# Nine changes of order and shape in a hand-scheduled attention-plus-mixer kernel

## The chip, the cores and the metric

The kernel runs on one core of one Trainium2 chip. The metric is device microseconds of one execution. A core has TensorE (PE; its weight loads are listed apart as PEld), VectorE (DVE), ScalarE (ACT), GpSimd (POOL) and SyncE (SP), which here only issues DMAs. Each engine works through its own list in order and waits on semaphores for the others.

## The reference

`B, H, S, D = 8, 8, 576, 64`, all inputs float32.

```python
def phi(x, c, s):                       # c, s: cos and sin of pi/2 * position / S
    r = np.maximum(x, 0.0)
    return np.concatenate([r * c, r * s], axis=-1)
q_p, k_p = phi(q, cos_w, sin_w), phi(k, cos_w, sin_w)
kv  = np.einsum('bhsf,bhsd->bhfd', k_p, v)
num = np.einsum('bhsf,bhfd->bhsd', q_p, kv)
den = np.einsum('bhsf,bhf->bhs', q_p, np.sum(k_p, axis=2))[..., None] + 1e-06
x   = (num / den).transpose(0, 2, 1, 3).reshape(B, S, H * D)      # 8 x 576 x 512

wq, wk = x @ w_q, x @ w_k                                        # 512 -> 64
W_tok  = 1 / np.sqrt(64) * np.einsum('bsd,btd->bst', wq, wk)
mixed  = np.einsum('bst,btd->bsd', W_tok, x)
out    = np.maximum(mixed, 0.0) @ w_out                          # 512 -> 512
```

The mixer is computed as wq times (wk-transposed times x), so that no 576 x 576 matrix is formed.

## The kernel before, in words

A batch is worked on in two *halves* of four heads, so there are 16 halves, H = 0 to 15; batch b has halves 2b and 2b+1. A half has two head pairs, and its results come in two groups g = 2H and 2H+1.

The program is one list of words, `ORDER`, read from left to right. Each word is one step, and its function has the word's letters as its name. A number behind the letters is the half, the group, the batch or the output tile; `a` and `b` are the two parts of a half; `:n` is the PSUM bank (of 8) that the step writes; `@A`, `@V`, `@G` put it on ACT, DVE or POOL. Nothing reorders the list: each engine gets its steps in the order of the list, and the framework adds the semaphore waits that data and buffers need. So a word further ahead on one engine changes nothing on another engine but what waits there.

The steps of a half, in the order of the data:

- `LK`, `LQ`, `LV` load k, q and v to five raw buffers each, all on SP's one queue, 288 KB a part. At most eight DMAs are on their way: a new one waits for the eighth before it. `ST` stores an output tile of 256 KB on the same queue, so a store whose tile isn't ready holds up the loads behind it.
- `RK`, `RQ` apply relu and give bf16. `CV` casts v, and `VS` (DVE) multiplies it with the cos/sin table; `VG` does both on POOL.
- `KV` sums k-transposed times v on PE, `KE` copies the sum to SBUF.
- `QT` transposes q on PE: for the halves in `QT_WIDE` with 9 transposes of 128 x 128, for the others with 18 of 64 rows by 64. `QM` (DVE) multiplies the result with the table into the operand of `N`: two instructions for a wide half, one for another.
- `N` multiplies with the sum of `KV` (20 small matmuls a group; five groups add epsilon with two more, line 348). `EP` adds epsilon, `RC` and `RJ` take reciprocals, `X` (DVE) writes x.
- `XT` (10 transposes of 128 x 128) or `XR` (20 of 64 rows) transposes x on PE, `XE` copies it out.

The steps of a batch: `WK`, `KW` (x times w_k and its copy), `WQ`, `QW` (the same for w_q), `KX`, `XK`, `XA`, `XB` (wk-transposed times x, its copy, and two copies across partitions), `MX`, `ME` (the mixing and its relu, four tiles a batch). Two batches give nine output tiles: `WO` (4 matmuls of 512 columns, line 509), `OE` (copy to SBUF), `ST`.

A `:n` of `QT`, `KV`, `N`, `XT`, `XR` and `MX` stands for the pair of banks n and n+1; `WK`, `WQ`, `KX` and `WO` take one bank. A step that writes a bank waits until the step that read its last content is done; so the bank number decides which engine a PE step waits for.

## Time and profile before

| | |
|---|---|
| median of 3 runs | 119.17 us (118.6 to 119.84) |
| the profiled execution | 118.42 us, of which the profile's span is 116.6 us; 1.8 us lie around it |
| PE busy | 94.7 us, 81% of the span, 2104 matmuls |
| DVE busy | 90.5 us, 78%, 162 instructions |
| ACT busy | 83.1 us, 71%, 147 instructions |
| POOL busy | 64.8 us, 56%, 65 instructions |
| DMA | 39.38 MB, mean 338 GB/s; loads 29.62 MB, stores 9.44 MB |
| granted TensorE clock | 0.9 or more in all 40 slices |

No engine is busy all the time. The page cuts the span in 40 slices of 2.9 us; in most of them two engines show eight tenths or more, and the DMA engines are at nine tenths in most of the first half. The chain of work that ended last tells which of them sets the end at each time; the timeline shows, for each instruction, how long its engine sat idle before it and who released it.

### The profile page before, as it was taken

To read this page: it belongs to the slowest core of one execution; us is meant where nothing else is said; L and a number is where in the kernel's file an instruction comes from. 1 tells how busy PE (TensorE), PEld (TensorE's weight loads), DVE (VectorE), ACT (ScalarE), POOL (GpSimd) and SP (SyncE) were. 2 spreads that over 40 slices of the span, in tenths; PEclk is the share of its full clock that TensorE was granted. 3 is DMA by queue.
4 is the path that set the end of the run, shared out by engine and by line. 5 is a ranking of instruction groups with operands and counts; after the bars stand their busy time and mean duration, and the time that the engine had idled before them with its cause. 6 is when DMAs were issued, how large, how long until landed. Compare 5 with 4: busy or idle time off the path is not lost.

```text
span 116.6 us, 4971 instructions
## 1 busy us (share of the span) xinstructions
PE 94.7 (81%) x2104; PEld 65.1 (56%) x2118; DVE 90.5 (78%) x162; ACT 83.1 (71%) x147; POOL 64.8 (56%) x65
## 2 busy tenths in 40 slices
PE   0005967779796797999999899999999999999970
PEld 0004856657576776647775656656775576463420
DVE  2008999799798999889799887898997996795620
ACT  4547558499899987898884878986888774546340
POOL 7600399861634796477298498899659901002000
PEclk9999999999999999999999999999999999999999
DMA  3999999999999999999979999987898467999874
GB/s 90 349 386 399 401 372 346 388 389 396 386 392 384 387 387 387 391 390 384 383 251 302 351 397 371 358 266 258 270 340 293 169 236 271 403 367 400 337 306 173
DMA packets 20662, 39.38 MB, mean 338 GB/s; under 512 B 3232, under 2 KB 3232, under 8 KB 20640
## 3 DMA queue, kind: packets, MB, share of 16 engines
q1 hardware_dynamic: 20640, 39.07, 92.4%
q8 instruction: 16, 0.26, 0.9%
q14 instruction: 6, 0.05, 0.1%
HBM read 29.62 MB, written 9.44 MB: 335 GB/s over the span
## 4 chain that ended last, share of the span: by engine, by line
PE 48%; DMA 26%; DVE 14%; SPq 4%; issue 3%; ACT 1%; DVEq 0%; ACTq 0%
PE ps L509 24%; DMA qraw<-in_q_dram 16%; DMA vraw<-in_v_dram 5%; DMA kraw<-in_k_dram 5%; PE ps L340 5%; DVE qm L316 5%; SPq L145 4%; PE ps L285 3%; PE ps L489 3%; PE ps L419 3%; PE ps L439 3%; DVE xT L213 3%; PE ps L466 3%; PE ps L452 2%; DVE x L393 2%
## 5 line engine op out<-in xcount | busy, mean ns | idle before, releaser
L248 POOL TENSOR_TENSOR v<-vraw,vtab 128x1152 bf16<-128x1152 f32 (+1 forms) x12 | 35.5, 2969 | 6.5 <-DVE qm L316 2.2
L509 PE MATMUL ps<-wow,mix 128*128 128x512 bf16 x130 | 33.3, 380 | 1.2 <-issue 0.3
L393 DVE TENSOR_TENSOR x<-ps,rec 128x640 bf16<-128x640 f32 x32 | 25.4, 818 | 0.7
L209 ACT COPY o<-ps 128x512 f32<-128x512 f32 x25 | 14.5, 592 | 9.2 <-PE ps L509 8.1
L509 PEld LDWEIGHTS <-mix 128*128 128x128 bf16 x144 | 12.5, 98 | 14.4 <-issue 1.7
L295 PE MATMUL ps<-ident,rq 128*128 128x128 bf16 x117 | 9.5, 233 | 12.0 <-ACT rq L203 11.0
L316 DVE TENSOR_TENSOR qm<-ps,qtab 128x1152 bf16<-128x1152 bf16 x26 | 18.3, 749 | 0.8 <-PE ps L295 0.7
L234 DVE TENSOR_TENSOR v<-vb,vtab 128x2304 bf16<-128x2304 bf16 (+1 forms) x11 | 11.8, 1084 | 7.7 <-ACT vb L209 7.3
L500 ACT ACTIVATE mix<-ps 128x576 bf16<-128x576 f32 x23 | 14.5, 651 | 3.5 <-PE ps L489 2.5
L340 PE MATMUL ps<-kvs,qm 64*128 64x65 bf16 x640 | 14.0, 193 | 2.1 <-ACT kvs L209 1.3
L295 PEld LDWEIGHTS <-rq 128*128 128x128 bf16 x117 | 7.6, 104 | 13.6 <-issue 10.5
L340 PEld LDWEIGHTS <-qm 64*128 64x128 bf16 x640 | 12.6, 96 | 4.2 <-issue 2.3
L203 ACT ACTIVATE rk<-kraw 128x1152 bf16<-128x1152 f32 (+1 forms) x14 | 14.0, 996 | 0.7 <-DMA kraw<-in_k_dram 0.7
L205 POOL TENSOR_SCALAR rq<-qraw 128x576 bf16<-128x576 f32 (+1 forms) x13 | 10.1, 776 | 4.4 <-DMA qraw<-in_q_dram 3.5
L211 POOL TENSOR_SCALAR vb<-vraw 128x576 bf16<-128x576 f32 (+1 forms) x7 | 5.7, 810 | 11.9 <-DMA vraw<-in_v_dram 8.8
L211 POOL TENSOR_SCALAR kx<-kx 64x256 bf16<-64x256 bf16 x9 | 4.1, 457 | 12.6 <-ACT kx L209 11.0
L502 DVE TENSOR_SCALAR mix<-ps 128x576 bf16<-128x576 f32 x9 | 6.8, 757 | 4.0 <-PE ps L489 3.8
L285 PE MATMUL ps<-v,rk 64*64 64x130 bf16 x432 | 9.1, 231 | 0.8 <-POOL v L248 0.7
L209 ACT CAST kvs<-ps 128x260 bf16<-128x260 f32 (+1 forms) x15 | 6.5, 436 | 4.6 <-PE ps L285 3.9
L285 PEld LDWEIGHTS <-rk 64*64 64x64 bf16 x432 | 7.5, 114 | 3.9 <-issue 1.2
L203 ACT ACTIVATE rq<-qraw 128x576 bf16<-128x576 f32 (+1 forms) x10 | 8.3, 832 | 1.1 <-DMA qraw<-in_q_dram 1.1
L213 DVE COPY xT<-ps 128x1280 bf16<-128x1280 bf16 (+1 forms) x9 | 7.3, 813 | 2.2 <-PE ps L419 2.0
(65 smaller groups left out, 137.3 us busy)
## 6 DMA issues: line engine op xcount, KB each, us to landing
kraw<-in_k_dram SPq DMA_DIRECT2D x32, 288.0 KB, 5.9
qraw<-in_q_dram SPq DMA_DIRECT2D x32, 288.0 KB, 5.9
vraw<-in_v_dram SPq DMA_DIRECT2D x32, 288.0 KB, 5.8
out_dram<-o SPq DMA_DIRECT2D x36, 256.0 KB, 3.4
wof<-in_moe_w_out_dram SPq DMA_DIRECT2D x4, 256.0 KB, 5.8
wkf<-in_moe_w_k_dram SPq DMA_DIRECT2D x1, 128.0 KB, 5.7
wqf<-in_moe_w_q_dram SPq DMA_DIRECT2D x1, 128.0 KB, 6.2
```

The costliest lines, as they stand in the source:

```text
L203: A.activation(dst, s, AF.Relu)
L209: A.copy(dst, s)
L213: V.tensor_copy(dst, s)
L234: V.tensor_mul(v2_b[H % NV2][:, part, :, :, 0:D], vb_b[H % NPREP][:, part].unsqueeze(3).to_broadcast([P, n, C, 2, D]), vtab.unsqueeze(1).t ...
L248: G.tensor_mul(dst[:, part, :, :, 0:D], s[:, part].unsqueeze(3).to_broadcast([P, n, C, 2, D]), vtab.unsqueeze(1).to_broadcast([P, n, C, 2, ...
L285: nc.tensor.matmul(kv_v[o, r, :], rk_of(H)[a, pr, c, :], v2_b[H % NV2][a, pr, c, :, 0:D + 1], start=(c == 0), stop=(c == C - 1))
L295: nc.tensor.transpose(qt_v[:, c, :], rq_b[H % NPREP][:, c, :, :], ident)
L316: V.tensor_mul(qm_b[H % NQM][:, :, r, 0:C, :], q_t[:, r].unsqueeze(1).to_broadcast([P, 2, C, H2]), qtab)
L340: nc.tensor.matmul(nv[:, pr, u, :], qm_b[H % NQM][a, s, r, 2 * u:2 * u + 2, :], kv_b[H % 2][a, r, pr if H in KV_WIDE else 0, s, 0:D + 1], ...
L393: V.tensor_tensor(x_b[b % NX][:, :, 4 * h:4 * h + 4, :].rearrange("p u (w r) d -> p r w u d", r=2)[:, r], nv[:, :, :, 0:D], rec(g).to_broa ...
L500: A.activation(dst, s, AF.Relu, scale=scale_moe)
L509: nc.tensor.matmul(o, mix_b[bp % 2][:, m, rt * P:(rt + 1) * P], wow[:, m, :], start=(m == 0), stop=(m == NDM - 1))
```

## The change

Nine edits, all in the list but the one in `QT_WIDE`:

1. `XR0:4` becomes `XT0:4`: 10 full transposes in place of 20 small ones for half 0.
2. `VS7` (one DVE instruction for both parts) becomes `VS7b VS7a` (two, the part that POOL casts first).
3. `WK2` moves from behind `N14` to ahead of `MX3` and `N14`, from bank 6 to bank 2. For this, `MX3` goes from bank 2 to 0, `N14` from 0 to 6, `WQ2` from 7 to 3, `KV6` from 2 to 0, and `N12` ahead of `N13`.
4. `MX9` moves behind `N16`.
5. `LQ12a` moves behind `ST11` on SP's queue.
6. `OE11` moves from DVE to ACT.
7. `XA3` and `QM11` move behind `KE11`, `XR9` and `XE8`; `XR9` goes from bank 4 to 0; `WO10` moves from ahead of `KV11` to behind `QT10`, from bank 1 to 4; `MX13` and `MX12` change banks.
8. `QT10` is no longer wide: 18 small transposes in place of 9, and `QM10` is one instruction.
9. `WK6` moves behind `WO25`, `KW6` behind `OE25`.

The line with most of the seventh edit, and the line of the eighth:

```diff
-LQ12b QT11:4 OE5:5@A RC19 RC18 X18 WO9:0 X19 WO10:1 OE9:7@A RQ10@G KV11:2 XA3@A QM11 XR8:6 KE11@A
-XR9:4 VG10a LV15a LV13a LQ14b LV14b LQ14a LV13b XE8@A QT10:2 XE9@V WO0:5 QM10 OE10:8@A MX13:0
+LV12b LK12b LQ12b QT11:4 OE5:5@A RC19 RC18 X18 WO9:0 X19 OE9:7@A RQ10@G KV11:2 XR8:6 KE11@A XR9:0
+VG10a LV15a LV13a LQ14b LV14b LQ14a LV13b XE8@A XA3@A QM11 QT10:2 WO10:4 XE9@V WO0:5 QM10 OE10:8@A
...
-    QT_WIDE = (0, 1, 2, 3, 4, 5, 6, 7, 8, 9, 10, 11, 14)
+    QT_WIDE = (0, 1, 2, 3, 4, 5, 6, 7, 8, 9, 11, 14)
```

Three places show what stands where. The first is PE's list where batch 2 begins. L340 is `N` (here group 14), L348 its epsilon, L439 `WK2`, L489 `MX3`; each pair of rows is shown once, however often it stands there. Before:

```order
L340 LDWEIGHTS qm_87
L340 MATMUL ps<-kvs_89,qm_87 128x65
L348 LDWEIGHTS ones
L348 MATMUL ps<-epsr,ones 128x5
L439 LDWEIGHTS xT_96
L439 MATMUL ps<-wkw,xT_96 128x64
```

And in the changed kernel, at the same place:

```order
L439 LDWEIGHTS xT_96
L439 MATMUL ps<-wkw,xT_96 128x64
L489 LDWEIGHTS kx_102
L489 MATMUL ps<-wq_100,kx_102 128x288
L340 LDWEIGHTS qm_87
L340 MATMUL ps<-kvs_89,qm_87 128x65
```

`WK2` has moved from the end of this stretch to its start, with `MX3` and then `N14` behind it.

The second place is around halves 10 and 11. On DVE, L393 is `X`, L378 `RC`, L316 a wide `QM`, L320 one that isn't wide, L213 a copy (`OE` into o, `XE` into xT), L502 `ME`:

```order
 L393 TENSOR_TENSOR x_94<-ps,rec_90 128x2x5x64
-L213 COPY o_112<-ps 128x512
 L378 RECIPROCAL rec_91<-rec_91 128x10 x2
 L393 TENSOR_TENSOR x_94<-ps,rec_91 128x2x5x64 x2
 L316 TENSOR_TENSOR qm_87<-ps,qtab 128x2x576 x2
 L213 COPY xT_96<-ps 128x2x2x5x64
-L316 TENSOR_TENSOR qm_86<-ps,qtab 128x2x576 x2
+L320 TENSOR_TENSOR qm_86<-ps,qtab 128x4x576
 L502 TENSOR_SCALAR mix_105<-ps 128x576
```

The copy `OE11` is gone from DVE, and `QM10` is one instruction. On ACT at the same place (L203 is `RQ11`; L209 are the copies `OE11`, `OE5`, `OE9` into o, `KE11` into kvs, `XE8` into xT and `XA3` within kx):

```order
 L203 ACTIVATE rq_81<-qraw_69 128x2x9x64
+L209 COPY o_112<-ps 128x512
 L209 COPY o_111<-ps 128x512
 L209 COPY o_113<-ps 128x512
-L209 COPY kx_103<-kx_103 64x256
 L209 CAST kvs_89<-ps 128x2x2x65
 L209 COPY xT_96<-ps 128x2x2x5x64
+L209 COPY kx_103<-kx_103 64x256
```

`OE11` stands here now, right behind `RQ11`, and `XA3` comes two copies later.

The third place is ACT's list near the end, where L203 is `RK15` and L209 are `OE25` (into o), `KW6` (into wk) and `KE15` (into kvs):

```order
 L357 ACTIVATE rec_92<-ps,eps 128x10
 L203 ACTIVATE rk_79<-kraw_63 128x1152
+L209 COPY o_121<-ps 128x512
 L209 CAST wk_98<-ps 128x320
-L209 COPY o_121<-ps 128x512
 L209 CAST kvs_89<-ps 128x2x2x65
```

`OE25` and `KW6` have changed places, as `WO25` and `WK6` have on PE.

## The prediction

> **What bounds the kernel now.** I read the page's DMA slices (40 of 2.9 us each) and the chain's shares first, then the chain of work that ended last in order of time (start, length, what), and the timeline where the chain changes engine.

> ```profile
> GB/s 90 349 386 399 401 372 346 388 389 396 386 392 384 387 387 387 391 390 384 383 251 302 351 397 371 358 266 258 270 340 293 169 236 271 403 367 400 337 306 173
> PE 48%; DMA 26%; DVE 14%; SPq 4%; issue 3%; ACT 1%; DVEq 0%; ACTq 0%
> ```

> ```profile
> 30.89 5.95 DMA qraw<-in_q_dram
> ...
> 44.66 0.74 PE ps L439 x20
> ...
> 66.06 0.83 DVE xT L213
> ...
> 107.72 5.30 PE ps L509 x24
> ...
> 113.04 0.59 ACT o L209
> ```

> The chain runs through loads until 36.84, and most slices there show 370 to 400 GB/s: until then the kernel takes what the queue brings. From 37 to 44.6 it is mostly DVE, from 44.66 to 113.0 mostly PE with a few stretches of DVE, such as the one at 66.06; the end is 24 matmuls of the last products in a row and one copy. So an edit before 37 us can give nothing at the end; one behind it gives what it takes from PE, or from a DVE stretch in which PE waits, and PE carries that to the end unless a load or another engine becomes late.

> **The change part by part.** Edit 1 lies at 20 us, ahead of loads that set the pace until 36.84: nothing. Should that cover be gone, PE would lose the difference of 10 large and 20 small transposes:

> ```profile
> 20.02 0.47 PE L419 MATMUL ps<-ident,x 64*128 64x64 bf16 x20
> 26.51 0.68 PE L406 MATMUL ps<-ident,x 128*128 128x128 bf16 x9
> ```

> That is 0.2 us at most.

> Edit 2, `VS7` in two.

> ```profile
> 35.51 0.67 POOL L211 TENSOR_SCALAR vb<-vraw 128x576 bf16<-128x576 f32 x1 [1.88 <-DVE rec L359]
> 36.40 0.67 ACT L209 CAST vb<-vraw 128x576 bf16<-128x576 f32 x1
> 37.59 1.36 DVE L234 TENSOR_TENSOR v<-vb,vtab 128x2304 bf16<-128x2304 bf16 x1 [0.42 <-ACT kvs L209]
> 43.19 1.42 DVE L316 TENSOR_TENSOR qm<-ps,qtab 128x1152 bf16<-128x1152 bf16 x2
> 44.52 0.75 DVE L234 TENSOR_TENSOR v<-vb,vtab 128x1152 bf16<-128x1152 bf16 x1
> ```

> DVE sat idle 0.42 us before `VS7`, from 37.17 on. `VS7` waits for both casts, POOL's (to 36.18) and ACT's (to 37.07). `VS7b` needs POOL's alone and can start at 37.17; `VS7a` follows with its cast done. Two pieces take 2 x 0.75 = 1.50 in place of 1.36: 0.14 more. The steps behind it on DVE, to `QM6` at 44.61, follow each other with gaps of a tenth at most, so it ends 0.42 - 0.14 = 0.28 us earlier. The bounds: the gap is put down to a kvs copy (`KE4`) that `VS7` does not read. If it is not the wait for a cast, it stays, and the edit costs 0.14. I take 0.25, nearer to the upper end, because the row shows an idle engine and `VS7b` waits for nothing of ACT's.

> [...]

> Edit 3, `WK2` ahead.

> ```profile
> 42.08 1.20 ACT L500 ACTIVATE mix<-ps 128x576 bf16<-128x576 f32 x2
> 43.08 0.49 PE L340 MATMUL ps<-kvs,qm 64*128 64x65 bf16 x20
> 44.66 0.74 PE L439 MATMUL ps<-wkw,xT 128*128 128x64 bf16 x20 [0.66 <-DVE qm L316]
> 45.33 0.68 PE L452 MATMUL ps<-xT,wqw 128*64 128x288 bf16 x8
> 45.44 1.55 DVE L393 TENSOR_TENSOR x<-ps,rec 128x640 bf16<-128x640 f32 x2
> ```

> PE stood still for 0.66 us until `QM6` freed bank 6. In bank 2 `WK2` waits for `ME7` (42.08 + 1.20 = 43.28) and starts behind `N15`, near 43.4; `MX3` follows and is done by 44.3. Now `N14` stands in banks 6 and 7 and waits for `QM6` in its place, until 44.65; 20 such matmuls add about 0.35 and its epsilon 0.1, so `WQ2` starts near 45.12 instead of 45.33: 0.21 us, and with the 0.25 of edit 2 in front 0.46. Should `WK2` itself wait in bank 2, up to 0.21 is lost; should `N14`'s matmuls hide behind it, up to 0.66 is won: I take the middle of the steps, which is worked out from their own rows. Behind the waiting `N14` are queued `WQ2`, `KV6` and `KX2`; and `KX2` in bank 7 now waits for `X14`, which reads `N14`. `X14` is the first of the pair at 45.44, ends near 46.25, and with edit 2 near 46.0; PE comes there at 44.87 + 0.68 and some 0.6 for `KV6`, near 46.15. No wait, but by a tenth only; if `X14` were late, each tenth is a tenth.

> Edit 4, `MX9` behind `N16`.

> ```profile
> 57.49 0.42 PE L489 MATMUL ps<-wq,kx 64*128 64x288 bf16 x4
> 58.02 0.76 DVE L502 TENSOR_SCALAR mix<-ps 128x576 bf16<-128x576 f32 x1 [0.58 <-PE ps L489]
> 58.88 0.40 ACT L209 CAST wq<-ps 128x288 bf16<-128x288 f32 x1 [0.40 <-PE ps L452]
> ```

> The first pair at 57.49 is `MX9`, which waited for `QM8`, and `MX11` stood behind it. `MX11` needs no `QM8`, so `ME11` on DVE loses part of its 0.58 of idle time; but DVE soon takes what PE's `N` give it. On PE it fills the tenth that it waited. 0.1 us, bounds 0 and 0.3. ACT's `ME9` comes some 0.3 later, which the 0.40 of idle time behind it takes up; without that cover `QW3` would be late by 0.3, and nothing needs it for some us.

> Edits 6, 7 and 8, around halves 10 and 11.

> ```profile
> 61.69 0.69 DVE L213 COPY o<-ps 128x512 f32<-128x512 f32 x1
> 62.52 0.59 ACT L209 COPY o<-ps 128x512 f32<-128x512 f32 x1 [0.83 <-PE ps L509]
> 65.95 0.68 PE L295 MATMUL ps<-ident,rq 128*128 128x128 bf16 x9
> 66.06 0.82 DVE L213 COPY xT<-ps 128x1280 bf16<-128x1280 bf16 x1 [0.56 <-PE ps L419]
> 66.93 1.02 PE L509 MATMUL ps<-wow,mix 128*128 128x512 bf16 x3 [0.31 <-DVE xT L213]
> 73.69 0.44 PE L301 MATMUL ps<-ident,rq 64*128 64x64 bf16 x18
> ```

> PE waited 0.31 us for `XE9`, because `WO0` shares its bank with `XR9`. Now `XR9` stands in bank 0 and comes 0.88 (one `WO`: 4 of the 24 matmuls in 5.30) earlier, as `WO10` no longer stands ahead of it; `X19`, which it needs, also comes 0.7 earlier, since `OE11` (0.69) has left DVE. ACT has room for it: it sat idle 0.83 right there, and the copy takes 0.59. `XE9` then runs beside `WO10`. PE gets the 0.31 back, and 0.68 - 0.44 = 0.24 from `QT10` in small transposes. 0.55 us; bounds 0.24 (the wait comes back elsewhere: `N22` needs `QM10`, which by my count ends a tenth before PE is there) and 0.7 (DVE's 0.69 in full).

> Edit 5, `LQ12a` behind `ST11`.

> ```profile
> 62.41 0.34 SPq L519 DMA_DIRECT2D out_dram<-o  x1
> 62.80 1.92 SPq L145 DMA_DIRECT2D kraw<-in_k_dram  x2
> 71.05 1.15 ACT L203 ACTIVATE rk<-kraw 128x1152 bf16<-128x1152 f32 x1
> kraw<-in_k_dram SPq DMA_DIRECT2D x32, 288.0 KB, 5.9
> ```

> SP moves it past one store and no more. Behind it are `LK12a` and `LK10b`: issued by 64.7, landing 5.9 later, about 69.4 to 70.6, for `RK10` at 71.05, which by then is wanted at 69.95. Cost 0 to 0.6 us; I take 0, since `ST11` itself goes out some 0.4 earlier and as many bytes stand ahead of `LK10b` as before.

> Edit 9, `WK6` and `WO25`.

> ```profile
> 93.13 1.16 ACT L203 ACTIVATE rk<-kraw 128x1152 bf16<-128x1152 f32 x1
> 94.19 0.43 ACT L209 CAST wk<-ps 128x320 bf16<-128x320 f32 x1
> 95.02 0.59 ACT L209 COPY o<-ps 128x512 f32<-128x512 f32 x1 [0.41 <-PE ps L509]
> 95.57 0.74 PE L466 MATMUL ps<-x,wk 128*64 128x256 bf16 x10
> ```

> PE does the same work in the two orders. `KW6` ends near 95.4 instead of 94.62, and `KX6` wants it at 95.57: 0, bounds 0 and 0.1 lost. `OE25` starts at 94.3, 0.7 earlier, and with it the stores queued behind `ST25`.

> **The sum**, against the profiled execution: 0.25 + 0.21 + 0.1 + 0.55 = 1.1 us, so 118.42 becomes 117.3. That execution lies 0.75 below the median of the runs, so I expect 119.17 - 1.1 = **118.1 us**. With each edit at its lower bound it would be -0.14 + 0 + 0 + 0.24 - 0.6 - 0.1 = 0.6 lost, with each at its upper bound 0.28 + 0.66 + 0.3 + 0.7 = 1.9 won.

> **The rivals.**

> *The store queue sets the end.* From `ST25` on 25 stores of 256 KB go out. At the 400 GB/s of slices 35 and 37 one takes 0.66 us, 25 take 16.4, and 95.6 + 16.4 = 112.0, with the last one issued at 113.6: 1.6 us of slack, more than the 1.1 gained, and edit 9 adds 0.7. If the stores need more than that, as the three slices of 337 and less at the end may hint, the end follows `OE25`: 1.1 + 0.7 = 1.8 us, 117.4 us. Against it: those slices are as slow as `WO` makes tiles, one of 262 KB in 0.88 us or 298 GB/s.

> [...]

> *Part of it dissolves.* `VS7`'s gap stays and the split costs 0.14, or ACT holds the gain to 0.5 from `RK10` on, because the k load is late; ACT has next to no idle time there to catch up:

> ```profile
> 72.00:76.00 4.00, 3.68 (x108) 2.36 (x108) 3.43 (x6) 3.95 (x10) 3.21 (x3) 1.00 0.96 364
> ```

> The columns are PE, PEld, DVE, ACT and POOL; ACT is busy 3.95 of 4 us. For it also speaks that the gap's releaser is not the cast. Then 0.4 to 0.7 is left: 118.6 us.

> *The change doesn't do what it says:* each wait comes back one step later, at `X14`, `QM10` and the loads of `VG11` and `RQ10`, which arrive when the queue brings them. 119.2.

> *Slower:* the load queue. The first k load behind a lone store took long to issue:

> ```profile
> 56.71 0.35 SPq L519 DMA_DIRECT2D out_dram<-o  x1
> 57.58 2.15 SPq L145 DMA_DIRECT2D kraw<-in_k_dram  x1
> ```

> If `LQ12a` behind `ST11` adds one such issue of 2.15, `LK10b` lands at 70.6 + 2.15 = 72.75, `RK10` and `KV10` start 1.7 later than now, and of the gain ahead of it nothing is left: 119.17 + 1.7 = 120.9. Against it: `ST11` goes out no later than now. It decides from a landing after 71.05.

> **How the numbers follow.** Chances: the sum 0.48 (117.6 to 118.4), part of it 0.25, the store queue 0.09, nothing 0.11, slower 0.07. No more than 2 in 10 may be left out, so the range reaches from the store queue's case with 0.3 to spare, 117.1, to the case of nothing with 0.3, 119.5; the slower case stays out. About 1% (1.2 us) is what a measurement of this kernel can tell from no change. Faster by more than that: the store queue's case (0.09) and somewhat more than half of the sum's, 1.1 against a bound of 1.2 with more room above (1.9), 0.27: 0.36 together. Slower by more: 0.07. Within 1%: 0.57.

> **What would show it.** In the profile after: no gap before the `VS` at 37.2, two of 0.75; no idle time before `WK2`'s matmuls, and a wait for DVE before `N14`; the 0.31 before `WO0` gone and 18 transposes of 0.44 for half 10; `OE25` starting right behind `RK15`; the last `WO` ending 1.1 earlier. I am wrong if `RK10` shows a wait for its load, if `KX2` waits for `X14`, or if the last stores land later behind the last copy than now.

## The result and the profile after

| | before | after |
|---|---|---|
| median of 21 runs each | 119.17 us (118.24 to 120.64) | 117.79 us (116.91 to 119.83) |
| ratio to before, 95% interval | | 0.9884 [0.9863, 0.9906] |
| the profiled execution, and its span | 118.42 and 116.6 us | 118.21 and 116.4 us |

The change makes the kernel 1.16% faster, 1.38 us; forecast were 1.1 us and 118.1. Ratios, here and below, leave out executions that took over 1.5% longer than the fastest of the same kernel, so that two of four are left in e10 and five of twelve in e11. The two profiled executions differ by only 0.2 us. A sum made against a profiled execution can't be read off the length of another one, so I compare stretches within each, and the times.

The page's chain shares, and five pieces of the chain of work that ended last (start, length, what), of the kernel after:

```profile
PE 49%; DMA 21%; DVE 18%; ACT 4%; issue 4%; SPq 1%; ACTq 0%; DVEq 0%
```

```profile
19.17 6.99 DMA vraw<-in_v_dram
...
44.78 0.47 PE ps L340 x20
...
57.39 0.51 issue
...
107.48 5.30 PE ps L509 x24
...
112.81 0.59 ACT o L209
```

The structure is that of before: loads, then DVE, then PE to the end. New is a piece in which PE waits for nothing that the profile shows ("issue"), at 57.39.

Now each place of the prediction, in the timeline after (start, length, engine, line, operation, count, and in brackets the idle time before it with its releaser). `VS7` first:

```profile
36.24 1.49 DVE L393 TENSOR_TENSOR x<-ps,rec 128x640 bf16<-128x640 f32 x2
36.89 0.67 ACT L209 CAST vb<-vraw 128x576 bf16<-128x576 f32 x1
37.65 1.42 DVE L234 TENSOR_TENSOR v<-vb,vtab 128x1152 bf16<-128x1152 bf16 x2
```

The two pieces follow `X11` at once and take 1.42 together, where the one took 1.36: 0.06 more, not 0.14. ACT's cast was done at 37.56, so the first piece does not run ahead of it; what the gap was, e1 takes up. Then `WK2`, `MX3` and `N14`:

```profile
43.62 0.76 PE L439 MATMUL ps<-wkw,xT 128*128 128x64 bf16 x20
44.31 0.30 PE L489 MATMUL ps<-wq,kx 64*128 64x288 bf16 x2
44.78 0.49 PE L340 MATMUL ps<-kvs,qm 64*128 64x65 bf16 x20 [0.18 <-DVE qm L316]
45.20 0.68 PE L452 MATMUL ps<-xT,wqw 128*64 128x288 bf16 x8
```

No idle time before `WK2`; the wait for `QM6` stands before `N14` and is 0.18 in place of 0.66. Halves 10 and 11:

```profile
64.28 0.72 PE L285 MATMUL ps<-v,rk 64*64 64x130 bf16 x36
65.53 0.44 PE L301 MATMUL ps<-ident,rq 64*128 64x64 bf16 x18
65.80 0.82 DVE L213 COPY xT<-ps 128x1280 bf16<-128x1280 bf16 x1 [0.27 <-PE ps L419]
65.90 1.90 PE L509 MATMUL ps<-wow,mix 128*128 128x512 bf16 x7
67.73 0.42 PE L489 MATMUL ps<-wq,kx 64*128 64x288 bf16 x4
```

From `KV11` to `MX13` PE shows no wait; the 0.31 before `WO0` is gone, and `XE9` runs beside `WO10`. Near the end `OE25` (0.59) comes right behind `RK15`, `KW6` behind it, and `KX6` is not held up:

```profile
92.85 1.16 ACT L203 ACTIVATE rk<-kraw 128x1152 bf16<-128x1152 f32 x1
94.16 0.59 ACT L209 COPY o<-ps 128x512 f32<-128x512 f32 x1
94.75 0.43 ACT L209 CAST wk<-ps 128x320 bf16<-128x320 f32 x1
95.33 0.74 PE L466 MATMUL ps<-x,wk 128*64 128x256 bf16 x10
```

What moved, step by step: the start of a step after, less its start before, in the two profiled executions.

| X11 | EP8 | QM6 | WQ2 | KX2 | N16 | WO9 | WO12 | KX5 | KX6 | last copy |
|---|---|---|---|---|---|---|---|---|---|---|
| +0.57 | +0.12 | +0.11 | -0.13 | -0.13 | +0.49 | +0.54 | -0.28 | -0.28 | -0.23 | -0.23 |

This execution came to `X11` 0.57 late with its loads (`LK7a` landed at 31.38, before at 30.84). From there the edits win 0.45, 0.24 and 0.82; 0.05 are lost at `KX6`. Between `KX2` and `N16`, where the list of PE changes little, 0.62 are lost, most of it in the "issue" piece. The experiments take the first three by themselves, undo single edits, and then turn to the loss.

### The profile page after: what moved, and what is told of

It reads as the page before. It is cut to its first block, busy times and chain, and to the rows that moved or that the text cites. A ratio compares the mean times of both kernels' runs of the same rounds, so it can differ in the third digit from the quotient of the medians.

```text
span 116.4 us, 4965 instructions
## 1 busy us (share of the span) xinstructions
PE 94.8 (81%) x2103; PEld 64.9 (56%) x2117; DVE 90.2 (77%) x161; ACT 83.7 (72%) x148; POOL 64.2 (55%) x65
## 4 chain that ended last, share of the span: by engine, by line
PE 49%; DMA 21%; DVE 18%; ACT 4%; issue 4%; SPq 1%; ACTq 0%; DVEq 0%
PE ps L509 24%; DMA vraw<-in_v_dram 10%; DVE qm L316 6%; DMA kraw<-in_k_dram 6%; DMA wkf<-in_moe_w_k_dram 5%; PE ps L340 5%; PE ps L285 5%; DVE x L393 4%; PE ps L489 3%; DVE v L234 3%; PE ps L419 3%; PE ps L466 3%; PE ps L452 2%; PE ps L439 2%; DVE xT L213 2%
## 5 line engine op out<-in xcount | busy, mean ns | idle before, releaser
L509 PE MATMUL ps<-wow,mix 128*128 128x512 bf16 x130 | 33.3, 380 | 0.9 <-issue 0.3
L393 DVE TENSOR_TENSOR x<-ps,rec 128x640 bf16<-128x640 f32 x32 | 25.4, 817 | 0.7
L209 ACT COPY o<-ps 128x512 f32<-128x512 f32 x26 | 15.1, 591 | 7.8 <-PE ps L509 6.8
L509 PEld LDWEIGHTS <-mix 128*128 128x128 bf16 x144 | 12.4, 98 | 14.1 <-issue 1.3
L295 PE MATMUL ps<-ident,rq 128*128 128x128 bf16 x108 | 8.8, 235 | 11.6 <-ACT rq L203 10.9
L234 DVE TENSOR_TENSOR v<-vb,vtab 128x1152 bf16<-128x1152 bf16 (+1 forms) x12 | 11.8, 1007 | 8.1 <-ACT vb L209 8.0
L316 DVE TENSOR_TENSOR qm<-ps,qtab 128x1152 bf16<-128x1152 bf16 x24 | 16.9, 749 | 0.5 <-ACT kvs L209 0.5
L500 ACT ACTIVATE mix<-ps 128x576 bf16<-128x576 f32 x23 | 14.6, 651 | 3.8 <-PE ps L489 2.8
L340 PE MATMUL ps<-kvs,qm 64*128 64x65 bf16 x640 | 14.0, 193 | 3.0 <-ACT kvs L209 2.6
L340 PEld LDWEIGHTS <-qm 64*128 64x128 bf16 x640 | 12.6, 96 | 5.1 <-issue 3.9
L203 ACT ACTIVATE rk<-kraw 128x1152 bf16<-128x1152 f32 (+1 forms) x14 | 14.0, 997 | 0.9 <-DMA kraw<-in_k_dram 0.6
L295 PEld LDWEIGHTS <-rq 128*128 128x128 bf16 x108 | 7.1, 105 | 13.1 <-issue 10.2
L211 POOL TENSOR_SCALAR vb<-vraw 128x576 bf16<-128x576 f32 (+1 forms) x7 | 5.7, 808 | 12.2 <-DMA vraw<-in_v_dram 9.1
L211 POOL TENSOR_SCALAR kx<-kx 64x256 bf16<-64x256 bf16 x9 | 3.6, 400 | 12.5 <-ACT kx L209 9.9
L502 DVE TENSOR_SCALAR mix<-ps 128x576 bf16<-128x576 f32 x9 | 6.8, 755 | 4.4 <-PE ps L489 4.3
L209 ACT CAST kvs<-ps 128x260 bf16<-128x260 f32 (+1 forms) x15 | 6.6, 437 | 4.6 <-PE ps L285 4.0
L203 ACT ACTIVATE rq<-qraw 128x576 bf16<-128x576 f32 (+1 forms) x10 | 8.3, 831 | 1.2 <-DMA qraw<-in_q_dram 1.1
L213 DVE COPY xT<-ps 128x1280 bf16<-128x1280 bf16 (+1 forms) x9 | 7.3, 807 | 1.6 <-PE ps L419 1.5
## 6 DMA issues: line engine op xcount, KB each, us to landing
kraw<-in_k_dram SPq DMA_DIRECT2D x32, 288.0 KB, 5.9
qraw<-in_q_dram SPq DMA_DIRECT2D x32, 288.0 KB, 5.9
vraw<-in_v_dram SPq DMA_DIRECT2D x32, 288.0 KB, 5.9
```

Of the source, the lines that this page charges most:

```text
L203: A.activation(dst, s, AF.Relu)
L209: A.copy(dst, s)
L234: V.tensor_mul(v2_b[H % NV2][:, part, :, :, 0:D], vb_b[H % NPREP][:, part].unsqueeze(3).to_broadcast([P, n, C, 2, D]), vtab.unsqueeze(1).t ...
L295: nc.tensor.transpose(qt_v[:, c, :], rq_b[H % NPREP][:, c, :, :], ident)
L316: V.tensor_mul(qm_b[H % NQM][:, :, r, 0:C, :], q_t[:, r].unsqueeze(1).to_broadcast([P, 2, C, H2]), qtab)
L340: nc.tensor.matmul(nv[:, pr, u, :], qm_b[H % NQM][a, s, r, 2 * u:2 * u + 2, :], kv_b[H % 2][a, r, pr if H in KV_WIDE else 0, s, 0:D + 1], ...
```

## The experiments

Every kernel was timed in turn with the kernel before, which ran 11 to 29 times beside it; ratios are to it, with 95% intervals. Stretches are from the start of one step to the start of another, on one profiled execution of each kernel. In the first four (`e1` to `e4`) the line numbers of the profile are two lower (L437 is `WK2`, L507 `WO`).

**e1: edit 2 alone, on the kernel before.**

```diff
-VS7 N8:2
+VS7b VS7a N8:2
```

> The kernel before with edit 2 alone: VS7 in two operations, everything else as before. Theory A (the chain goes on from DVE to PE, and what DVE gains at 37 us reaches the end): the gap of 0.42 us before VS7 goes, the two pieces cost at most 0.14 more than the one, so 0.25 to 0.45 us less at the end, ratio 0.996 to 0.998. Rival B (a late load or another wait behind it takes the gain back): the gap is gone in the trace, but the time is that of before, ratio 0.999 to 1.001. Rival C (the op count): no gap less, 0.14 us more, ratio 1.001.

0.9967 [0.9933, 1.0], 0.4 us. In its timeline the gap is gone:

```profile
35.56 1.49 DVE L391 TENSOR_TENSOR x<-ps,rec 128x640 bf16<-128x640 f32 x2
36.97 1.42 DVE L232 TENSOR_TENSOR v<-vb,vtab 128x1152 bf16<-128x1152 bf16 x2
```

From the start of `X11` to that of `EP8`, the step behind `VS7`, it is 2.06 us, as after; before it is 2.51. From `N16` to the end this execution stays 0.38 to 0.42 ahead of the one of before, 0.11 of it from ahead of `X11`. Theory A fits, and C is out: the gap is gone. The interval reaches 1.0, so the times alone do not exclude B.

The split removes the gap, but the reason that the prediction gave for it does not hold. In the three profiles with `VS7` in one piece (before, e2, e3) ACT's cast ended 0.10, 0.10 and 0.17 ahead of the end of `X11`, so DVE did not stand idle for the cast; the prediction's own rows show this too (37.07 against 37.17). `KE4`, the releaser shown, is doubtful as well:

```profile
37.31 1.36 DVE L232 TENSOR_TENSOR v<-vb,vtab 128x2304 bf16<-128x2304 bf16 x1 [0.39 <-ACT kvs L207]
```

This is e2, where `KE4` ended at 37.31 too, and `VS7` does not read what it writes. `VS7` starts 0.49 to 0.52 behind the end of the cast in all three. What it stood for in that time stays open.

**e2: edit 3 alone, on the kernel before.**

```diff
-N15:4 QM6 RK6a@A MX3:2 N14:0
+N15:4 WK2:2 QM6 RK6a@A MX3:0 N14:6
...
-RK6b@A WK2:6 ME3@A
+RK6b@A ME3@A
```

> The kernel before with edit 3 alone: WK2 ahead of MX3 and N14, with its banks. Theory A: WQ2 starts 0.2 to 0.25 us earlier, and as PE is on the chain from there, 0.2 us less at the end, ratio 0.998. Rival B: the next wait takes it back (KX2 for X14, or the late loads of half 9), ratio 1.000. The trace must show no idle time before WK2's matmuls and a wait for DVE before N14's.

0.9992 [0.9956, 1.0028]: this can't tell 0.2 us from none. The trace can, for the place: from `QM6` to `WQ2` 1.89 us, after 1.90, before 2.14, in e1 (without this edit) 2.15. So 0.25 is won there, and `KX2` waits for nothing. Whether it reaches the end the times leave open. In this execution it does not: PE is level with before again at `KV9`, and later it loses 1.0 in half 14:

```profile
87.78 0.67 POOL L203 TENSOR_SCALAR rk<-kraw 128x576 bf16<-128x576 f32 x1 [3.98 <-ACT xT L207]
90.32 0.25 PE L283 MATMUL ps<-v,rk 64*64 64x130 bf16 x4 [0.78 <-issue]
```

POOL's cast of half 14's k came at 87.78, where it was 85.34 before (its load landed at 87.61, before at 85.17). But `KV14` started only 0.08 later than before, at 88.88. What is lost is the 0.78 for which the last four matmuls of that sum waited, without a releaser.

**e3: edits 6, 7 and 8 alone, on the kernel before.** The diff is that of the change, with `OE11` on ACT.

> The kernel before with edits 6, 7 and 8 alone: OE11 on ACT, XR9, WO10, XA3 and QM11 in the new order with their banks, QT10 in small transposes. Theory A (this is the largest part): the 0.31 us before WO0 go, QT10 takes 0.24 less, in all 0.55 to 0.8 us less at the end, ratio 0.993 to 0.995. Rival B (the wait comes back behind it, at N22 for QM10 or at RK10 for its load): 0.2 us, ratio 0.998.

0.9951 [0.9911, 0.999], 0.6 us: theory A's size, though the interval takes in B's 0.998. The trace decides for the place. From `WO9` to `WO12` PE takes 5.12 us, as after; before it is 5.94. So 0.82 is won at the place.

**e5 and e6: what in it does it.** The changed kernel, once with `OE11` back on DVE, once with half 10 wide again.

```diff
-OE11:6@A
+OE11:6@V
```

> The changed kernel with edit 6 undone: OE11 on DVE again. Theory A (X19, XR9 and XE9 come 0.7 us earlier because OE11 left DVE, and the 0.31 us before WO0 hang on it as much as on the order): XE9 ends too late for WO0 again or X19 holds PE, 0.2 to 0.6 us lost, ratio to before 0.990 to 0.994. Rival B (the new order alone gives the 0.31 us, since XR9 comes 0.88 us earlier and WO10 stands ahead of WO0): ratio 0.988 as with the whole change.

```diff
-    QT_WIDE = (0, 1, 2, 3, 4, 5, 6, 7, 8, 9, 11, 14)
+    QT_WIDE = (0, 1, 2, 3, 4, 5, 6, 7, 8, 9, 10, 11, 14)
```

> The changed kernel with edit 8 undone: half 10 transposed with 9 wide transposes, QM10 in two instructions. Theory A (the step of the prediction): 9 wide transposes take 0.24 us more of PE, which is on the chain there, ratio to before 0.990 to 0.991. Rival B: PE has that time, or it is taken up by a wait behind it (N22 for QM10), ratio 0.988.

e5: 0.9935 [0.9901, 0.9968], 0.6 us worse than the whole change. `WO9` to `WO12` takes 5.63, 0.51 more, and the row of `KV11` says why:

```profile
63.57 1.41 DVE L316 TENSOR_TENSOR qm<-ps,qtab 128x1152 bf16<-128x1152 bf16 x2
63.71 0.72 PE L285 MATMUL ps<-v,rk 64*64 64x130 bf16 x36 [0.45 <-DVE x L393]
64.95 0.44 PE L301 MATMUL ps<-ident,rq 64*128 64x64 bf16 x18
```

`KV11` writes the bank that `X19` reads, and with `WO10` moved away nothing stands between. So in the new order it is `OE11`'s 0.68 us on DVE that would hold PE, at `KV11` and not at `WO0`: theory A, by the second of the two waits that it named (`X19` holds PE). e6: 0.9891 [0.9849, 0.9934], which includes both expectations; the stretch takes 5.34, 0.22 more, for 0.24 expected.

```profile
64.91 0.68 PE L295 MATMUL ps<-ident,rq 128*128 128x128 bf16 x9
67.25 0.42 PE L489 MATMUL ps<-wq,kx 64*128 64x288 bf16 x4
```

**e4: edit 9 undone.**

```diff
-RC29 X29 WO25:2 QM15 WK6:3 OE25:15@A
+WK6:3 RC29 X29 WO25:2 KW6@A QM15 OE25:15@A
```

> The changed kernel with edit 9 undone: WK6 ahead of WO25 and KW6 ahead of OE25 again. Theory A (PE sets the end, edit 9 is worth nothing on it and costs up to 0.1 us at KX6): 117.7 to 117.8 us, ratio to before 0.987 to 0.989. Rival (the queue of stores sets the end, and the 0.7 us by which OE25 came earlier is what the change gained): 118.4 to 118.5 us, ratio 0.994, and the wait of OE28 for its store grows by about 0.25 us with no effect on the last product.

0.9846 [0.9795, 0.9898]: no loss, so the store queue does not set the end. In the traces the last store lands 3.9 us after the last `WO` starts, before, after and in e4 alike.

**e7: edit 5 undone.**

```diff
-LV10b KV8:0
+LV10b LQ12a KV8:0
```

> The changed kernel with edit 5 undone: LQ12a ahead of the store of tile 11 again. Theory A (no cost and no gain): ratio to before 0.988, and RK10 without a wait for its load. Rival B (the load of half 10, which landed at 68.83 in the changed kernel and 69.39 in the one before, would come late for RK10 now that it starts earlier): up to 0.6 us lost, ratio 0.992 to 0.993.

0.9889 [0.9843, 0.9935]: theory A's value, but the interval takes in B's 0.992. The trace speaks against B. In the kernel after `LK10b` landed at 68.83, and `RK10` at 70.76 followed the work ahead of it on ACT without idle time; in e7's profile, of an execution of 124.58 us, the load landed at 74.16 and `RK10` started at 76.47, again with no idle time ahead of it.

### The wait that no row releases

In the kernel after, these are PE's matmuls and weight loads of halves 8 and 9 (`KV8` and `KV9`, 36 each):

```profile
56.19 1.21 PE L285 MATMUL ps<-v,rk 64*64 64x130 bf16 x69 [0.25 <-DVE qm L316]
56.19 1.07 PEld L285 LDWEIGHTS <-rk 64*64 64x64 bf16 x69 [0.22 <-issue]
57.91 0.25 PE L285 MATMUL ps<-v,rk 64*64 64x130 bf16 x3 [0.51 <-issue]
57.91 0.11 PEld L285 LDWEIGHTS <-rk 64*64 64x64 bf16 x2 [0.65 <-issue]
```

Two weight loads are left when PE stops for 0.65 us. In e1, whose list is 10 pairs (weight load and matmul) longer ahead of it, there are 12 left:

```profile
55.49 1.07 PEld L283 LDWEIGHTS <-rk 64*64 64x64 bf16 x60 [0.42 <-issue]
56.75 0.22 PEld L283 LDWEIGHTS <-rk 64*64 64x64 bf16 x12 [0.19 <-issue]
```

Counted from the start of the trace, both stop before weight load 989 (counting from 0). The matmuls' other stops of 0.2 us and more without a releaser, behind 37 us in all the profiles, are at 861, 1117, 1373 and 1756 or 1757: multiples of 128 apart, up to one, and 128 pairs are 256 instructions. The page lists a queue that fits:

```profile
q8 instruction: 16, 0.26, 0.9%
```

16 packets of 16 KB, for 16.5 times 256 instructions on PE (2117 weight loads and 2103 matmuls). In the traces of before and of after one of them begins behind each number 93 + 128n of the weight loads (93 to 2013, 16 in all), ahead of the next such number. In the trace of after the packet ahead of that stop was under way from 55.47 to 56.58, and PE went on at 57.91, 1.3 later. In all fourteen profiles the matmuls' stops of 0.25 us and more that have no releaser, behind 37 us, stand at these numbers and end 1.2 to 1.6 us after such a packet. The execution of before had this packet at 53.07 to 54.20 and no stop, nor had e2.

**e8: fewer instructions ahead.** The changed kernel with two halves more in `KV_WIDE`.

```diff
-    KV_WIDE = (2, 4, 5, 7)
+    KV_WIDE = (1, 2, 3, 4, 5, 7)
```

> The changed kernel with halves 1 and 3 summed by 18 wide matmuls in place of 36 (the flag that halves 2, 4, 5 and 7 have): the same result, 36 pairs of instructions fewer on PE, 0.57 us more of PE's time for each of the two, both where loads set the pace. It is for a stall that no step of mine has: in the profile of the changed kernel PE stands still for 0.65 us in half 9's sum at weight load 989, without a releaser, and in two kernels whose list is 10 pairs longer ahead of that place at the same number 989, 10 pairs earlier in the work; each time it ends 1.3 to 1.5 us after a packet of 16 KB of the instruction queue was through. Theory F (PE waits there for its own instructions, at a fixed number of them): the stall leaves half 9's sum, number 989 now lies 36 pairs later in the work, and PE reaches it 0.4 to 0.6 us later, so it shrinks to 0 to 0.2 us, and the time falls by up to 0.5 us, ratio to before 0.984 to 0.988. Rival G (half 9's sum waits for its k, cast on POOL): the stall stays in half 9's sum, ratio 0.988 or more.

0.9979 [0.9943, 1.0015]. The place is as F says: all 72 weight loads of halves 8 and 9 in one row, and the stop 36 pairs later in the work, in `WQ3`, at number 988:

```profile
56.17 1.30 PEld L285 LDWEIGHTS <-rk 64*64 64x64 bf16 x72 [0.42 <-issue]
58.31 0.38 PEld L452 LDWEIGHTS <-wqw 128*64 128x64 bf16 x7
59.26 0.11 PEld L452 LDWEIGHTS <-wqw 128*64 128x64 bf16 x1 [0.56 <-issue]
```

The size was not: the kernel got slower by 1% against the whole change, not faster. The packet came later too (56.97 to 57.87, 2.3 us after PE had entered the block ahead). I had moved the boundary without asking how fast PE runs through the new 128 pairs. Where the whole 1% went I did not settle. The two wide sums, at the 0.57 us more each that I had taken as hidden behind loads, would make 1.1 us, which is the size of it; no run tells them from the stops. In this profile `X11` is not late (36.57, after 36.92), and 0.7 us are lost from `X11` to `KV8` (19.60 against 18.94).

**e10: the same, done properly.** 24 matmuls that nobody reads, while PE has nothing to do; the sizes come from the time that PE takes for each 128 pairs.

```diff
-LK2b TB TI
+LK2b TB WU97:7 TI
```

> The changed kernel with 24 matmuls more that nobody reads, behind the program's first memsets: PE stands still until 9.9 us there, and they are done by about 8 us, so they cost PE nothing. They only shift which instruction has which number: 24 pairs. Theory A (no step of the prediction knows of it): the time of the changed kernel, ratio to before 0.988. Theory F (PE waits for its instructions at numbers 93 + 128n): the numbers now fall 24 pairs earlier in the work, between a run of small matmuls and the next; from the times of the weight loads in the profile of the changed kernel it loses 2.2 us near number 861 (half 7's transposes to half 8's), 1.9 us near 1117 (halves 10 and 11) and 0.7 us near 2013, some of it taken up by waits that are there anyway: 2 to 4 us slower than the changed kernel, ratio to before 1.005 to 1.022, and the stalls at weight loads 861 and 1117.

1.0111 [1.0043, 1.018]: 2.3% or 2.7 us slower than the changed kernel, by work that was done at 9.3 us, ahead of PE's first own step. The two executions behind the ratio took 120.08 and 120.17 us, the other two 123.07 and 123.21. The profile is of the one of 123.21, so its stops do not add up to the 2.7. The stop at 861:

```profile
1.45 7.86 PE L548 MATMUL ps<-warm 64*128 64x384 bf16 x24 [1.45 <-DVE warm L539]
9.99 1.12 PE L295 MATMUL ps<-ident,rq 128*128 128x128 bf16 x9 [0.68 <-ACT rq L203]
...
50.69 0.82 PE L509 MATMUL ps<-wow,mix 128*128 128x512 bf16 x3 [2.31 <-issue]
```

2.31 us where 2.2 were expected; at 1117 it was 0.3 where 1.9 were, and at 1756 it was 1.15 that I had not. So the numbering alone cost 2.7 us here; which boundaries stop PE, and for how long, differs between the profiles.

**e9, e11 and e12: a better numbering?** The changed kernel with edit 1 undone (10 pairs more ahead), with edits 1 and 9 undone, and with half 2 also transposed by 10 large transposes (10 pairs fewer).

```diff
-XT0:4
+XR0:4
...
-XR2:2
+XT2:2
```

> The changed kernel with edit 1 undone: half 0 transposed by 20 small transposes again. Theory A (the prediction: it lies ahead of loads that set the pace, so it is worth nothing): ratio to before 0.988, as with the whole change. Theory F (PE waits for its own instructions at every 128th weight load when it has run through the 128 before in less than about 5.8 us): the 10 pairs more put number 989 ten pairs earlier in half 9's sum; worked out from the times of PE's weight loads in the profiles of five kernels with a wait of 3.3 us for the packet while loads run, this alters the time by between 0.3 us lost and 0.9 won, mostly won: ratio 0.981 to 0.991.

> The changed kernel with edits 1 and 9 undone, the two that the runs so far show no gain of, as a version that may beat both: theory A 0.987 to 0.988 (edit 9 cost 0.05 us at KX6 in the profile), theory F 0.981 to 0.990.

> The changed kernel with half 2 transposed by 10 transposes of 128 x 128 in place of 20 small ones (what edit 1 does for half 0), at 32 us, where loads set the pace. It takes 10 pairs of instructions off PE, so that every 128th weight load falls ten pairs later in the work; number 989 then lies behind half 9's sum, and not in it. A version that may beat both kernels. Theory F: worked out from the weight loads of four profiles of the changed kernel and its variants, the stalls fall from 0.6 to 1.4 us to 0.4 to 0.7 us, so 0.2 to 0.6 us less: ratio to before 0.983 to 0.987. Theory A (the place of the numbers doesn't matter at this size): ratio 0.988.

0.9913 [0.9878, 0.9948], 0.9918 [0.9867, 0.9968] and 0.9887 [0.9829, 0.9945]. None differs from the whole change by what can be measured, so no version is shown to beat it. e11 is the weakest of the three: the median of all its twelve executions is 119.25 us, against 119.37 of the kernel before beside it. F's sizes of a few tenths were not borne out: in e9 PE's weight loads stopped at 989 again (0.38) and at 1756 (0.56), in e11 not there but PE stopped for 0.84 us at 1117, in e12 for nothing above 0.2 at either, and its profiled execution is the shortest of all (span 115.2). A model with one delay for all packets found the stop of 2 us in e10, missed another there by 1.6, and says nothing about tenths.

## Why the prediction was right, and where its terms were off

- **Edit 1**, taken as nothing: no difference shown (e9). "Loads set the pace there" was right, but the reason was not complete, since the edit also moves the numbers of all later instructions on PE.
- **Edit 2**, 0.25: measured 0.45 at the place. That the gap would go was right; the reason was not shown. The argument was the wait for ACT's cast, and the cast was over before the gap began; what the gap was stays open (e1). That part is luck. What was mis-sized is the cost of the second operation: 0.06 (1.42 against 1.36), not the 0.14 of two durations added, since the two pieces overlap by 0.08 (0.75 each, 1.42 together); and `VS7b` starts 0.08 ahead of the end of `X11`. The 0.06 stand against an idle time of 0.42.
- **Edit 3**, 0.21: measured 0.24 and 0.25. `KX2` did not wait for `X14`, by 0.05 (46.46 and 46.41). The best-founded term, worked out step by step from rows.
- **Edit 4**, 0.1: in two variants of the changed kernel with no stop in half 9 (e5, e11) `KV9` to `KX3` takes 1.84 and 1.88, before 1.92: 0.04 to 0.08. From `KX3` to `WO9` e5 takes 4.11, before 4.18, so 0.15 in all. In the profile after, the stop covers it. No run has this edit by itself.
- **Edits 6 to 8**, 0.55 with an upper bound of 0.7: measured 0.82. `QT10` was right (0.22 for 0.24). The 0.31 before `WO0` was the wrong measure for the rest, 0.6: it is what was left of DVE's lateness behind a `WO10` that stood ahead of `KV11` and covered it. `OE11`'s move by itself is worth 0.51 (e5); the last 0.09 no run takes apart.
- **Edits 5 and 9**, 0 and at most 0.1 lost: no loss shown for either. The 0.05 at `KX6` is not edit 9's: from `KV15` to `KX6` it is 0.69 after and in e11, where edit 9 is undone, and 0.64 or 0.65 in the twelve other profiles, seven of them with edit 9.
- **The sum**, 1.1: the stretches give 0.45 + 0.24 + 0.15 + 0.82 = 1.7; the times show 1.4. e1, e2 and e3, each alone, add up to 0.4 + 0.1 + 0.6 = 1.1, with intervals of some 0.4 each; whether the rest comes from the other edits stays open. That the forecast came so near is in part luck: two terms were too small by 0.2 and 0.27, and no term stood for PE's stops without a releaser. What those take from the times on average, before and after, is not shown.
- **The rivals.** The store queue: out (e4). Part of it dissolves: not by `VS7`'s gap, which is gone (0.42 before, none after), and not by `RK10`; but 0.62 of it was lost between `KX2` and `N16` in the profiled execution, most of it by the stop in half 9, which no rival named. Slower by SP's queue: `LK10b` was issued in 0.44 us, not 2.15.
- **The last `WO`** ended 0.23 earlier in the profile, not 1.1; the late loads (0.57) and the 0.62 ahead of `N16` account for the difference.

## What to carry to other kernels

Price an edit by a stretch between two steps that both kernels have, in several executions: the stretches here repeat to 0.1 us where no late load and no stop without a releaser falls into them (`QM6` to `WQ2` 1.89 and 1.90, `WO9` to `WO12` 5.12 twice), while the 21 executions of the kernel after lie between 116.91 and 119.83 us. When work leaves an engine, count what it frees at each later wait for that engine, in the new order and not in the old one. Look at the instruction's number where a wait has no releaser. Here it stayed 988 or 989 while the work moved past it by 10 pairs (e1) and by 36 (e8), and 24 pairs added at 1.45 us brought a stop of 2.31 at 861 (e10): an edit far ahead that adds or drops instructions can move such a stop, and how fast the engine runs through the 128 pairs ahead belongs in the estimate.

## What the runs showed of the hardware

- The instruction queue moved 16 packets of 16 KB in before and in after, one begun behind each number 93 + 128n of PE's weight loads (93 to 2013). Where PE's matmuls stopped without a releaser, in ten of the fourteen profiles, they went on 1.2 to 1.6 us after such a packet, and the packet came up to 4.7 us after PE's entry into the 128 pairs ahead (3.33 and 1.63 at the stop's place in after and before). The stops are of 0.22 to 2.31 us, at numbers 128 weight loads apart.
- Behind the stop of 2.31 us in e10 the granted TensorE clock fell to half for 3.4 us, 51.41 to 54.83 (columns: window, us, busy time and count of PE, PEld, DVE, ACT and POOL, granted clock, DMA share, GB/s):

```profile
50.00:52.00 2.00, 1.11 (x4) 0.56 (x6) 1.46 (x2) 1.26 (x4) 1.70 (x3) 0.85 1.05 394
52.00:54.00 2.00, 2.00 (x6) 0.61 (x4) 0.00 (x0) 0.50 (x1) 1.18 (x2) 0.50 1.06 390
54.00:56.00 2.00, 2.00 (x26) 0.69 (x26) 0.76 (x1) 1.49 (x3) 0.67 (x1) 0.79 1.03 387
```

  e7's profile shows a second such stretch, from 30.72 to 34.13 (five tenths in the page's slice from 30.70 to 33.77), behind a wait of PE for DVE of 1.32 us that ended at 30.55. But behind its longer wait of 2.44 us, which ended at 45.47, the clock stayed at 1.00 (44:46 and 46:48):

```profile
44.00:46.00 2.00, 0.53 (x10) 0.53 (x11) 1.93 (x6) 0.18 (x1) 0.62 (x1) 1.00 1.01 373
46.00:48.00 2.00, 2.00 (x33) 1.53 (x30) 1.93 (x4) 1.26 (x3) 0.00 (x0) 1.00 0.96 346
```

  So the length of one stop does not decide it; what does stays open.
